# Attention and two MLPs on one core: tiles' homes in SBUF moved by steps of 32 bytes

## The chip, the cores and the metric

One core of a Trainium2 chip. The metric is device time in microseconds (us), the median of several executions. Engines: TensorE (PE; its weight loads are PEld), VectorE (DVE), ScalarE (ACT), GpSimd (POOL), and SyncE (SP), which issues the DMAs.

## The reference

Local attention over chunks of 32 queries (16 keys to the left, 8 to the right, 8 memory keys), then two MLPs over the 3072 tokens.

```python
scores = scale * np.matmul(q_c, k_full.transpose(0, 1, 3, 2))
...
x = np.ascontiguousarray(attn_out.transpose(0, 2, 1, 3)).reshape(B * S, H * D)
x = _moe_ref(x=x, **moe_kwargs)            # h = x @ w_in; g = silu(h); g @ w_out
return _moe2_ref(x=x, **moe2_kwargs)       # h = x @ w_in; g = relu(h)**2; g @ w_out
```

d_model is 512, d_ff is 2048, all in float32.

## The kernel before

Every float32 operand of the MLPs is kept as a high and a low part (fp32r), and a product is three matmuls: low by high, high by low, high by high. In each matmul one operand is *held* (128x128, loaded into the array) and one is *moving* (128 rows by 256 or 512 columns). In `nc.tensor.matmul(out, a, b)` a is held and b is moving.

Tokens are worked on in six blocks of 512. Blocks 0 and 1 go through the first MLP plainly: the hidden matmuls hold w_in (tiles i and d) under the moving tokens x0 or x1 (even blocks in x0, odd ones in x1); the back matmuls (`mlp`, lines 1250 to 1252) hold w_out (tiles o and u) under moving g. Blocks 2 to 5 have the same hidden matmuls, while the second half of the first MLP is done by a scheme with seven products of half-size blocks in place of eight; `multiply` (line 1585) issues them, with w held and g moving. The second MLP uses the seven-product scheme in both halves, for 48 pairs of weight blocks over six token blocks: `visit` (line 1403) multiplies the weight forms (held; tiles i, d, o and u2) with forms of the tokens (moving; tiles rv, rv, rq and four in x1), and `multiply` has g held and w moving (tiles wraw and wu; the fourth product in x0). Hidden matmuls: 6 blocks x 16 x 12 = 1152 of 512 columns, half of them in even blocks. Of the products over one pair of weights, 42 matmuls, 12 are over rv, 6 over rq and 24 over x1.

`multiply` swaps the two operands for the first layer:

```python
held, moving = g[:, at, a], w[:, wat, c]
if layer == 0:
    held, moving = moving, held
```

The order of all instructions on every engine is written out in ORDER; no planner runs.

Each tag has a pool, and pools stand in SBUF one behind the other in the order in which they are opened, each as long as its number of buffers times its largest tile. Slices of a tile used by a matmul start at multiples of 512 bytes from the tile's start. So where a tile starts, modulo some power of two, is set by the pools before it. Before: u0, u1, u2 (8320 bytes each), a gap of 64 bytes, then rq, pr, pts, xq, x0, x1, wraw, wu, wr, y (all multiples of 2048 bytes), a gap of 64, then i, d, o, g (multiples of 4096), rv (two of 4160), nm, sm. Homes in bytes modulo 256, from the start of the first pool, before and after the change:

```
tile                       before   after
rq                          192       32
x1, odd token blocks        192       96   (starts 64 into its tile)
x1, second MLP's tokens     192       32
x0                          192      128
wraw, wu                    192        0
i, d, o                       0      128
u0, u2                        0      128
u1                          128        0
g                             0       32
rv, first of a block          0       64   (starts 64 into its tile)
rv, second                   64       64

moving over held           before   after   (moving minus held, -128 to 128)
hidden, even: x0 over i, d  -64        0
hidden, odd: x1 over i, d   -64      -32
back: g over o, u0, u2        0      -96
back: g over u1             128       32
first-layer out: g over o     0      -96
first-layer out: g over x0   64      -96
products: x1, rq over forms -64      -96
products: first rv            0      -64
products: second rv          64      -64
second-layer out: wraw, wu over g  -64  -32
second-layer out: x0 over g       -64   96
```

Of the kernel before, what the change touches and what calls it, by code (L numbers as in the profile page):

```python
# [12 lines left out]
F32 = mybir.dt.float32  # L13
F32R = mybir.dt.float32r
# [15 lines left out]
TB = UG * GQ  # L30
# [4 lines left out]
P = 128  # L35
KT = DM // P
# [22 lines left out]
HALF2 = T2 // 2  # L59
# [11 lines left out]
WARM, DENSE = 512, 9  # L71
KEEP = 0
PLAIN, OUTS = 2, 10

# [249 lines left out]
def chunk_attention_two_mlps(ctx, tc, head, units, weights, out):  # L326
# [3 lines left out]
    def pool(tag, n=1, space=None):  # L330
        kw = {} if space is None else {"space": space}
        bufs[tag] = n
        pools[tag] = ctx.enter_context(tc.tile_pool(name=tag, bufs=n, **kw))
        return pools[tag]
# [1 line left out]

    moving = (
        ("rq", 1), ("pr", 1), ("pts", 1), ("xq", 3), ("x0", 1), ("x1", 1), ("wraw", 2),  # L340
        ("wu", 4), ("wr", 3), ("y", 2),
    )
    held = [(f"i{i}", 1) for i in range(FT) if i not in JOINED]
    held += [(f"d{i}", 1) for i in range(len(JOINED) // 2)] + [(f"o{i}", 1) for i in range(OUTS)]

    def gap(tag):
        pool(tag).tile([P, 16], F32, tag=tag, name=tag)

    for tag in ("u0", "u1", "u2"):
        pool(tag)  # L350
    gap("gap0")
    for tag, n in moving:
        pool(tag, n)
    gap("gap1")
    for tag, n in (*held, ("g", 3), ("rv", 2), ("nm", 3), ("sm", 4)):
        pool(tag, n)
    for tag, n in (("acc", 4), ("ph", 2), ("sc", 2)):
        pool(tag, n, bass.MemoryType.PSUM)
# [9 lines left out]
    def f(ap):  # L368
        return ap.bitcast(F32)

    def take(b, shape, dtype, name=None):
        b.tile = pools[b.tag].tile(shape, dtype, tag=b.tag, name=name or b.tag)
        return b.tile
# [22 lines left out]
    a = G.add({"DVE": 0.3}, -100.0, fill, new=[ones])  # L396
    a = G.add({"PE": 3.9}, -100.0, warm, [a], new=[dense], uses=[ones])
# [14 lines left out]
    for n in range(KEEP):  # L412
        a = G.add({"PE": 0.45}, 100.0, keep, [a], uses=[dense, ones])
# [12 lines left out]
    def step_due(j, i):  # L426
        if j == 0:
            return FIRST + SLOW * i / FT
        if j < PLAIN:
            return FIRST + SLOW + (j - 1) * BLOCK1 + i * STEP1  # L430
        return FIRST + SLOW + (PLAIN - 1) * BLOCK1 + (j - PLAIN) * BLOCKW + i * BLOCKW / FT
# [374 lines left out]
    def split_x(j, p, po, done, due):  # L806

        new = []
        if j not in x_buf:
            x_buf[j] = G.buf(f"x{j % 2}")  # L810
            x_done[j] = []
            new = [x_buf[j]]
        xb = x_buf[j]

        def tokens(c):
            t = xb.tile[:, c, p]
            return t if j < ON_PE else t.rearrange("p (g c q) -> p g c q", g=UG, c=GC)

        def made():
            return po.tile if j < ON_PE else po.tile.rearrange("p c g q -> p g c q")  # L820

        def x_high(e):
            if new:
                take(xb, [P, 2, KT, TB], F32R)
            nc.scalar.copy(tokens(0), made())  # L825

        def x_low(e):
            nc.vector.tensor_tensor(tokens(1), made(), f(tokens(0)), op=ALU.subtract)  # L828

        a = G.add({"ACT": 0.60}, due - 1, x_high, [*done, *x_done[j]], new=new, uses=[po, xb])  # L830
        x_done[j].append(G.add({"DVE": 0.7}, due, x_low, [a], uses=[po, xb],
                               port=j >= ON_PE))
# [470 lines left out]
    def tokens(b, due):  # L1303

        t0 = b * T2
        after, xf = stored[b], G.buf("x0")
        loads = []

        def form(n):
            return xf.tile[:, n]  # L1310

        for n, (k, half) in enumerate(((0, 0), (2, 0), (2, 1), (0, 1))):
            def load(e, n=n, k=k, half=half):
                if n == 0:
                    take(xf, [P, 7, 2, HALF2], F32, "xf")
                at = t0 + half * HALF2
                nc.sync.dma_start(
                    out=xf.tile[:, n],
                    in_=y1[k:k + 2, :, at:at + HALF2].rearrange("k p t -> p k t"),
                )  # L1320

            p = G.add({"SP": 0.45}, due - 50 + n, load, after, new=[xf] * (n == 0),
                      uses=[xf] * (n > 0), size=P * T2 * 4)
            p.behind += loads[:1]
            p.release = due - 50
            loads.append(p)

        def sums(o, a, b, after, at):
            def emit(e):
                engine[e].tensor_tensor(form(o), form(a), form(b), op=ALU.subtract)  # L1330

            p = G.add({"DVE": 0.70, "POOL": 1.30}, at, emit, after, uses=[xf], port=True)
            p.release = due - 40
            return p

        b11, b21, b22, b12 = loads
        t1 = sums(4, 3, 0, [b12, b11], due - 20)
        t3 = sums(3, 2, 3, [b22, t1], due - 18)
        t2 = sums(5, 2, 4, [b22, t1], due - 18)
        t4 = sums(6, 5, 1, [t2, b21], due - 16)  # L1340
        ready = {0: b11, 1: b21, 2: b22, 3: t3, 4: t1, 5: t2, 6: t4}
        xs, four = {}, []
        need = [1.5 * rank for rank in range(7)]
        for rank, n in enumerate(X_FORM[p] for p in PRODUCTS):

            shared, at = rank > 2, max(0, rank - 3)
            new = not four or not shared
            if shared:
                four = four or [G.buf("x1")]
                x = four[0]  # L1350
            else:
                x = G.buf(("rv", "rv", "rq")[rank])

            def high(e, n=n, x=x, new=new, shared=shared, at=at):
                if new:
                    take(x, [P, 4 if shared else 1, 2, 2, HALF2], F32R, "xs")
                nc.scalar.copy(x.tile[:, at, 0], form(n))

            def low(e, n=n, x=x, at=at):
                t = x.tile[:, at]  # L1360
                engine[e].tensor_tensor(t[:, 1], form(n), f(t[:, 0]), op=ALU.subtract)

            a = G.add({"ACT": 0.60}, due - 3 + need[rank], high,
                      [ready[n]] + ([] if new else [x.by]),
                      new=[x] * new, uses=[xf] + [x] * (not new))
            xs[n] = (x, at, G.add({"DVE": 0.70, "POOL": 1.30}, due - 2 + need[rank], low, [a],
                                  uses=[xf, x], port=True))
        return xs
# [579 lines left out]
    for j in range(PLAIN):  # L1948
# [3 lines left out]
        else:  # L1952
# [4 lines left out]
            for k in range(PAIRS):  # L1957
                at = step_due(j, 1) + k * 11 * STEP1 / PAIRS
                convert_out(0, k, at)
                if k in WORK0:  # L1960
                    what, m = jobs.pop(0)
                    what(m, at + 10)
        y, rest = mlp(j)
# [89 lines left out]
```

## Time and profile before

| | |
|---|---|
| median of 3 runs | 1060.7 us (1060.2 to 1060.95) |
| the profiled execution | 1067.14 us |
| its span, first to last instruction | 1065.3 us |
| PE busy | 1051.2 us, 99% |
| PEld busy | 960.8 us, 90% |
| DVE busy | 827.3 us, 78% |
| ACT busy | 600.4 us, 56% |
| POOL busy | 266.9 us, 25% |
| mean granted TensorE clock | 0.997 |

Engines work side by side, so the shares add to more than one. Matmuls are pipelined: the next starts long before the last has ended, and a busy PE need not be at its peak.

### The profile page before, as it was taken

What the parts mean: (1) busy time and instruction counts of PE and PEld (TensorE: products, weight loads), DVE (VectorE), ACT (ScalarE), POOL (GpSimd) and SP (SyncE); (2) the same over time, 40 slices, a digit from 0 to 9 for tenths busy, and PEclk for the clock granted to TensorE, in tenths of its full rate; (3) what the DMA queues carried; (4) which work ended last, traced back from release to release, by engine and by line L of the source; (5) the groups of instructions that cost most, each with busy time, mean ns of one, the idle gap of its engine ahead of it and who ended that gap; (6) DMA issues with size and microseconds to landing.
All of it is one profiled execution on the core that took longest, in us unless ns stands there. A gap on an engine that the chain in (4) does not pass through costs nothing.

```text
span 1065.3 us, 24883 instructions
## 1 busy us (share of the span) xinstructions
PE 1051.2 (99%) x9801; PEld 960.8 (90%) x9801; DVE 827.3 (78%) x1608; ACT 600.4 (56%) x1106; POOL 266.9 (25%) x246
## 2 busy tenths in 40 slices
PE   7999999999999999999999999999999999999998
PEld 5778777778888888988989999999999999999998
DVE  6779767667888788897888877777777778777766
ACT  4898755557676777766567544335335334335333
POOL 3231123132334332420210321221221222221210
PEclk9899999999999999999999999999999999999999
DMA  8777686989798879887674875766776667667675
GB/s 292 272 246 229 227 283 226 294 258 318 238 306 279 281 257 303 279 305 248 212 233 145 275 222 181 247 215 201 241 218 210 210 215 221 205 210 226 200 237 176
DMA packets 139603, 256.80 MB, mean 241 GB/s; under 512 B 12128, under 2 KB 52192, under 8 KB 139488
## 3 DMA queue, kind: packets, MB, share of 16 engines
q1 hardware_dynamic: 139488, 255.23, 73.5%
q8 instruction: 77, 1.26, 0.5%
q14 instruction: 38, 0.31, 0.1%
HBM read 202.75 MB, written 52.43 MB: 240 GB/s over the span
## 4 chain that ended last, share of the span: by engine, by line
PE 91%; DVE 3%; DMA 3%; ACT 2%; issue 1%; POOL 0%; SPq 0%; DVEq 0%; ACTq 0%
PE out L1585 35%; PE pp L1403 20%; PE ph L1191 8%; PE ph L1192 8%; PE ph L1193 8%; PE acc L1250 3%; PE acc L1252 3%; PE acc L1251 3%; PE sc L519 1%; PE po L737 1%; DVE g L1465 1%; DMA xf<-y 1%; DMA blocks<-head 1%; DMA i<-weights 1%; DMA w2s<-ws 1%
## 5 line engine op out<-in xcount | busy, mean ns | idle before, releaser
L1403 PE MATMUL pp<-xs,forms 128*128 128x256 f32 x2016 | 269.2, 279 | 1.4 <-DVE kept L1429 1.0
L1585 PE MATMUL out<-w,g 128*128 128x256 f32 x2016 | 264.4, 278 | 0.1
L1403 PEld LDWEIGHTS pp<-xs,forms 128*128 128x128 f32 x2016 | 249.8, 188 | 2.3 <-DVE kept L1429 2.2
L1585 PEld LDWEIGHTS out<-w,g 128*128 128x128 f32 x2016 | 246.8, 188 | 0.3 <-DVE g L1465 0.3
L1461 ACT CAST g<-sums 128x512 fp32r<-128x512 f32 x240 | 148.0, 619 | 118.7 <-PE out L1585 91.5
L1465 DVE TENSOR_TENSOR g<-sums,g 128x512 fp32r<-128x512 f32 x201 | 155.1, 776 | 35.7 <-ACT g L1461 34.4
L1585 PE MATMUL out<-g,w 128*128 128x256 f32 x1344 | 173.3, 284 | 1.1 <-POOL g L1465 0.9
L1585 PEld LDWEIGHTS out<-g,w 128*128 128x128 f32 x1344 | 166.9, 191 | 6.2 <-POOL g L1465 1.1
L1420 ACT ACTIVATE sums<-pp 128x256 f32<-128x256 f32 x192 | 73.9, 385 | 160.2 <-PE pp L1403 120.5
L1446 POOL TENSOR_TENSOR sums<-sums 128x256 f32<-128x256 f32 x68 | 59.6, 880 | 289.9 <-DVE sums L1446 234.8
L1191 PE MATMUL ph<-x,i 128*128 128x512 f32 x240 | 96.9, 404 | 2.1 <-ACT x L825 1.9
L1192 PE MATMUL ph<-x,i 128*128 128x512 f32 x240 | 96.0, 400 | 0.5 <-DVE x L828 0.5
L1193 PE MATMUL ph<-x,i 128*128 128x512 f32 x240 | 95.6, 398 | 0.0
L1439 DVE SCALAR_TENSOR_TENSOR sums<-sums 128x256 f32<-128x256 f32 x144 | 69.0, 484 | 20.3 <-ACT sums L1420 18.7
L1465 POOL TENSOR_TENSOR g<-sums,g 128x512 fp32r<-128x512 f32 x39 | 51.1, 1313 | 103.2 <-ACT g L1461 103.0
L1446 DVE TENSOR_TENSOR sums<-sums 128x256 f32<-128x256 f32 x172 | 70.8, 431 | 5.7 <-ACT sums L1543 4.7
L1642 ACT CAST w<-w 128x512 fp32r<-128x512 f32 x100 | 59.1, 619 | 24.0 <-PE out L1585 18.1
L1648 DVE TENSOR_TENSOR w<-w,w 128x512 fp32r<-128x512 f32 x88 | 62.5, 736 | 10.0 <-ACT w L1642 9.1
L1429 DVE TENSOR_TENSOR sums<-pp,sums 128x256 f32<-128x256 f32 x96 | 40.2, 419 | 24.1 <-PE pp L1403 23.7
L1191 PEld LDWEIGHTS ph<-x,i 128*128 128x128 f32 x240 | 45.5, 190 | 13.7 <-ACT x L825 2.3
L1191 PE MATMUL ph<-x,d 128*128 128x512 f32 x144 | 57.7, 401 | 0.0
L1192 PE MATMUL ph<-x,d 128*128 128x512 f32 x144 | 56.8, 395 | 0.0
(136 smaller groups left out, 1574.8 us busy)
## 6 DMA issues: line engine op xcount, KB each, us to landing
w<-w2s SPq DMA_DIRECT2D x120, 512.0 KB, 4.0
w<-w1s SPq DMA_DIRECT2D x32, 768.0 KB, 5.2
w<-w2s SPq DMA_DIRECT2D x96, 256.0 KB, 3.3
wraw<-weights SPq DMA_DIRECT2D x44, 512.0 KB, 5.0
raw<-units SPq DMA_DIRECT2D x20, 768.0 KB, 5.7
w2s<-ws SPq DMA_DIRECT2D x56, 256.0 KB, 3.2
raw<-units SPq DMA_DIRECT2D x20, 520.0 KB, 6.0
bounce<-squares SPq DMA_DIRECT2D x32, 256.0 KB, 4.0
```

The costliest lines, as they stand in the source:

```text
L1191: nc.tensor.matmul(o, w[:, 1, ws], x[:, 0, kt], start=(kt == 0), stop=False)
L1192: nc.tensor.matmul(o, w[:, 0, ws], x[:, 1, kt], start=False, stop=False)
L1193: nc.tensor.matmul(o, w[:, 0, ws], x[:, 0, kt], start=False, stop=(kt == KT - 1))
L1403: nc.tensor.matmul(o[:, at], w[:, a, ws], t[:, c, kt], start=first and kt == 0 and r == 0, stop=kt == 1 and r == 2, skip_group_check=True,)
L1420: nc.scalar.activation(t[:, to], q.bank[bank].tile[:, h], func)
L1439: nc.vector.scalar_tensor_tensor(t, t, 0.0, t, op0=ALU.max, op1=ALU.mult)
L1446: engine[e].tensor_tensor(q.t.tile[:, to], a[0].tile[:, a[1]], b[0].tile[:, b[1]], op=op)
L1461: nc.scalar.copy(take(g, [P, 2, 2, HALF2], F32R, "g2")[:, :, 0], read())
L1465: engine[e].tensor_tensor(t[:, :, 1], read(), f(t[:, :, 0]), op=ALU.subtract)
L1585: nc.tensor.matmul(out_, held[:, ms], moving, start=first and r == 0 and (m == 0 or alone is not None), stop=last and r == 2, skip_group_c ...
L1642: nc.scalar.copy(take(w, [P, m, 2, HALF2], F32R, "w2")[:, :, 0], raw.tile[:, at:at + m])
L1648: engine[e].tensor_tensor(t[:, :, 1], raw.tile[:, at:at + m], f(t[:, :, 0]), op=ALU.subtract)
```

## The change

The pools are opened in another order, with one gap of 32 bytes in place of two of 64; the tokens of odd blocks start 64 bytes into a tile that is 96 bytes longer; and the first rv of a token block starts 64 bytes into its tile, which is no longer than the largest of its tag. No instruction is added, removed or moved in the order.

```diff
+GAP, STEP = 8, 24
...
-    moving = (
-        ("rq", 1), ("pr", 1), ("pts", 1), ("xq", 3), ("x0", 1), ("x1", 1), ("wraw", 2),
-        ("wu", 4), ("wr", 3), ("y", 2),
-    )
     held = [(f"i{i}", 1) for i in range(FT) if i not in JOINED]
     held += [(f"d{i}", 1) for i in range(len(JOINED) // 2)] + [(f"o{i}", 1) for i in range(OUTS)]
 
-    def gap(tag):
-        pool(tag).tile([P, 16], F32, tag=tag, name=tag)
-
-    for tag in ("u0", "u1", "u2"):
-        pool(tag)
-    gap("gap0")
-    for tag, n in moving:
+    for tag, n in (("wraw", 2), ("wu", 4), ("wr", 3), ("y", 2), ("pr", 1), ("pts", 1), ("xq", 3)):
         pool(tag, n)
-    gap("gap1")
-    for tag, n in (*held, ("g", 3), ("rv", 2), ("nm", 3), ("sm", 4)):
+    pool("gap").tile([P, GAP], F32, tag="gap", name="gap")
+    for tag, n in (
+        ("g", 3), ("rq", 1), ("x1", 1), *held, ("x0", 1), ("u0", 1), ("u1", 1), ("u2", 1), ("rv", 2),
+        ("nm", 3), ("sm", 4),
+    ):
         pool(tag, n)
...
         def x_high(e):
-            if new:
+            if new and xb.tag == "x1":
+                t = take(xb, [P, STEP + 2 * KT * TB], F32R)[:, 16:16 + 2 * KT * TB]
+                xb.tile = t.rearrange("p (a k t) -> p a k t", a=2, k=KT)
+            elif new:
                 take(xb, [P, 2, KT, TB], F32R)
...
                 if new:
-                    take(x, [P, 4 if shared else 1, 2, 2, HALF2], F32R, "xs")
+                    m, step = 4 if shared else 1, 16 * (rank == 0)
+                    t = take(x, [P, step + m * 4 * HALF2], F32R, "xs")[:, step:]
+                    x.tile = t.rearrange("p (n a k t) -> p n a k t", n=m, a=2, k=2)
```

## Rows read from the trace of the kernel before

**Rows 1.** The page: busy time by engine, and the chain by engine.
```profile
PE 1051.2 (99%) x9801; PEld 960.8 (90%) x9801; DVE 827.3 (78%) x1608; ACT 600.4 (56%) x1106; POOL 266.9 (25%) x246
...
PE 91%; DVE 3%; DMA 3%; ACT 2%; issue 1%; POOL 0%; SPq 0%; DVEq 0%; ACTq 0%
```

**Rows 2.** Waits of PE: total us, times, longest; the longest in total.
```profile
PE sc L605 <- DMA blocks<-head: 1.9, 3, 0.9
...
PE ph L1191 <- ACT x L825: 1.9, 1, 1.9
```

**Rows 3.** Three stretches: length, then busy us (instructions) of PE, PEld, DVE, ACT, POOL.
```profile
396.00:581.00 185.00, 185.00 (x1495) 164.73 (x1494) 155.93 (x288) 126.53 (x236) 39.75 (x36) 1.00 0.75 250
581.00:822.00 241.00, 240.61 (x2067) 239.95 (x2066) 188.38 (x377) 109.20 (x227) 58.17 (x49) 1.00 0.68 218
822.00:1065.00 243.00, 238.51 (x2059) 237.92 (x2057) 179.68 (x358) 96.48 (x199) 49.99 (x44) 1.00 0.68 214
```

**Rows 4.** Groups by line and form: count, busy us, mean ns, idle before.
```profile
L1403 PE MATMUL pp<-xs,forms 128*128 128x256 f32 x2016 | 269.2, 279 | 1.4 <-DVE kept L1429 1.0
L1585 PE MATMUL out<-w,g 128*128 128x256 f32 x2016 | 264.4, 278 | 0.1
...
L1585 PE MATMUL out<-g,w 128*128 128x256 f32 x1344 | 173.3, 284 | 1.1 <-POOL g L1465 0.9
```

**Rows 5.** The chain in order of time: start us, us, line, merged count.
```profile
502.40 4.31 PE out L1585 x36
...
613.38 2.12 PE pp L1403 x18
...
668.66 2.13 PE pp L1403 x18
...
672.20 2.83 PE out L1585 x24
...
679.97 1.41 PE out L1585 x12
...
682.10 1.38 PE out L1585 x12
...
684.87 1.36 PE out L1585 x12
...
692.35 2.10 PE pp L1403 x18
...
746.18 2.10 PE pp L1403 x18
...
749.64 2.72 PE out L1585 x24
...
753.04 2.04 PE out L1585 x18
...
787.98 0.39 ACT sums L1420
...
794.92 0.97 PE pp L1403 x6
```

**Rows 6.** Timeline of PE: hidden matmuls, first and last of 22 in a row.
```profile
507.02 0.39 PE L1193 MATMUL ph<-x,i 128*128 128x512 f32 x1
...
511.92 0.39 PE L1193 MATMUL ph<-x,i 128*128 128x512 f32 x1
```

**Rows 7.** Timeline of PE: back matmuls, of 24 over u1, of 12 over o7.
```profile
206.04 0.40 PE L1250 MATMUL acc<-g,u 128*128 128x512 f32 x1
...
211.39 0.40 PE L1252 MATMUL acc<-g,u 128*128 128x512 f32 x1
...
233.03 0.39 PE L1250 MATMUL acc<-g,o 128*128 128x512 f32 x1
...
235.52 0.39 PE L1252 MATMUL acc<-g,o 128*128 128x512 f32 x1
```

**Rows 8.** DMA issues: queue, count, KB each, median us to landing.
```profile
raw<-units SPq DMA_DIRECT2D x20, 768.0 KB, 5.7
```

More of the change, by code (lines that the diff above doesn't have):

```diff
@@ L1352, in tokens, with high @@
                 x = G.buf(("rv", "rv", "rq")[rank])
-            def high(e, n=n, x=x, new=new, shared=shared, at=at):
+            def high(e, n=n, x=x, new=new, shared=shared, at=at, rank=rank):
                 if new:
-                    take(x, [P, 4 if shared else 1, 2, 2, HALF2], F32R, "xs")
+                    m, step = 4 if shared else 1, 16 * (rank == 0)
+                    t = take(x, [P, step + m * 4 * HALF2], F32R, "xs")[:, step:]
+                    x.tile = t.rearrange("p (n a k t) -> p n a k t", n=m, a=2, k=2)
                 nc.scalar.copy(x.tile[:, at, 0], form(n))
```

## The prediction

> **What bounds the kernel now.** Read first the page's busy shares and the chain that ended last [rows 1]: PE is busy in 99% of the span, and 91% of the chain runs through it. The longest of PE's waits is 1.9 us [rows 2], and the stretches show PE busy in all of 396 to 581 us and in nearly all from 581 us on [rows 3]. So there is next to no idle time to win; what can change is the time from one matmul's start to the next, which I call its pace. The groups [rows 4] give counts and shapes, but no pace: their 278 ns is the pipelined length of one. The pace stands in the chain, where consecutive matmuls are merged: a piece's time through its count.
>
> For 128x256 matmuls there are three paces. A piece of first-layer output matmuls, g over held w, takes 4.31 us for 36, 119.7 ns each [rows 5]. A piece of second-layer output matmuls, w over held g, takes 1.41 us for 12 in one place, 117.5 ns, and 1.36 us for 12 a little later, 113.3 ns; twenty-four take 2.83 or 2.72 us, 117.9 or 113.3 ns each [rows 5]. The instructions are the same kind and shape, and nothing waits in these pieces. Of the products, L1403, a pair issues eighteen in a row over rv, rv and rq: they take 2.12 or 2.13 us in a slow stretch and still 2.10 in a quick one, where eighteen output matmuls take 2.04 [rows 5]. Either pace is kept: of the eighteens, the seven in the chain from 613.38 to 668.66 us are all slow, the six from 692.35 to 746.18 all quick.
>
> For 128x512 the hidden matmuls start 4.90 us apart over 21 steps, 233.3 ns each [rows 6]. The plain back matmuls take 2.49 us over 11 steps, 226.4 ns, with an o tile held; but 24 over u1 take 5.35 us over 23 steps, 232.6 ns [rows 7].
>
> Now lay the homes table of the kernel's section beside this, with distance = moving home minus held home, on a circle of 256 bytes. The pace 119.7 belongs to 0, 113.3 and 117.5 belong to -64, the slow eighteen have one third each at 0, +64 and -64. At 512 columns 0 has 226.4, -64 has 233.3, and u1, the only held tile at 128, has 232.6 where the o tile at 0 has 226.4. That u1 differs is why I keep 256 bytes and a sign, not 128: on a circle of 128 u1 would be at 0 too. The weights of the next matmul are loaded while this one streams (PEld is busy 237.92 of 243 us, [rows 3]), so both read SBUF together, and where they start seems to set how often they meet. The paces are read from rows; that distance is their cause is inferred, since the stages differ in more than that.
>
> **The change, part by part.** No instruction is added or dropped: the order is written out, the queues keep every DMA, no wait is new. Two views into longer tiles cost nothing. The whole sum is homes. What a distance not seen so far (-96, -32) costs I bound by the lowest and highest pace seen at that width.
>
> 1. First-layer output, g over w: 0 to -96. Of the 1344, 48 hold x0 and are left aside: 1296. The nearest row is -64, with 113.3 and 117.7 (the mean of 117.5 and 117.9); I take the middle, 115.5. (119.7 - 115.5) x 1296 = -5.4 us; ends 113.3 and 119.7: -8.3 to 0.
> 2. Second-layer output, w over g, 2016: -64 to -32 (288 of them, over x0, to +96). The present mean first: the last two stretches hold 4126 matmuls in 479.12 us of busy PE [rows 3], 116.1 ns each; 576 of those are over rv, at about 118 (that is 2.10 us less six of rq at 113.3, through 12), which leaves 115.8 for the others. -32 lies as near to 0 as to -64, so I take the middle of the ends 113.3 and 119.7: 116.5, or +0.7 x 2016 = +1.4 us; ends -5.0 to +7.9.
> 3. Products over x1 and rq, 1440: -64 to -96. Nearest is where they are: 0 us; ends 113.3 and 119.7: -3.6 to +5.6.
> 4. Products over rv, 576: 0 and +64 both to -64, a distance that has rows: 118 to 115.8, -1.3 us; ends -2.7 to 0.
> 5. Hidden, 576 in even token blocks: -64 to 0. At 0 the back matmuls show 226.4 in a stretch that keeps its pace; that every stretch does I don't assume, and count 229: (233.3 - 229) x 576 = -2.5 us; ends -4.0 and 0.
> 6. Hidden, 576 in odd blocks: -64 to -32, the middle of 226.4 and 233.3, 229.9: -2.0 us; ends -4.0 and 0.
> 7. Plain back, 384: 0 to -96, between -64 (233.3) and 128 (232.6), so about 233 for the 229 above: +1.5 us; ends 0 and +1.7. The 48 of them over u1 go to +32 and are counted with the rest.
>
> Sum -5.4 + 1.4 + 0 - 1.3 - 2.5 - 2.0 + 1.5 = -8.3 us. The profiled execution took 1067.14 us, 1.84 of them outside its span; it stands 6.4 us above the median of the runs, 1060.7. It would go to 1058.8, and the median to 1052.4.
>
> What takes a part back: PE in time needs its operands in time. DVE is busy 155.93 of 185 us in the first layer and less after that [rows 3], so a pace 3% quicker leaves it room. At the starts of token blocks the chain leaves PE for about 7 us, from ACT at 787.98 to the products at 794.92 [rows 5], while PE works on; a PE 1% quicker there arrives 0.1 us too soon, at each of five token blocks. I count nothing; without that cover it is 0.5 us. The raw loads now land in rq 32 bytes past a multiple of 64; they are due 50 us or more ahead in the code and take 5.7 us [rows 8], so even twice that would be covered.
>
> **A rule against it.** The row first: 119.7 ns against 113.3 for one shape, both without a wait [rows 5]. The Trainium skill ("TensorE: Matmul & The Clock Gate", Step-by-step: what each phase is for) says that TensorE has two independent SBUF read ports and that loading the next weights doesn't steal read bandwidth from the running matmul. By that rule alone homes would not matter, and the time would stay at 1060.7. The trace speaks against it without refuting it, since other things than homes differ between these stages.
>
> **The rivals.** *A, the quick pace everywhere.* The new distances let all 128x256 matmuls settle at 113.3: the low ends of 1, 2 and 3 are -8.3 - 5.0 - 3.6 = -16.9, with 4 to 7 as counted (-4.3) -21.2 us, 1039.5. For it: 113.3 exists, is held over many pairs, and once a slow stretch turned quick inside a run with no wait (1.41, 1.38, 1.36 for 12, [rows 5]). Against: two distances must both do it.
>
> *B, 32 bytes from 0 is as bad as 0.* -32 and -96 lock at 119.7 like the first layer's output. Then 1 gains nothing, 2 and 3 lose 7.9 and 5.6, and with -4.3 the sum is +9.2: 1069.9. For it: the only neighbour at 32 bytes of -32 on one side is the worst pace seen. Against: no row of -32 or -96 exists. With L the common pace of the 4752 matmuls of 1 to 3, the sum is zero where 1296 (L - 119.7) + 2016 (L - 115.8) + 1440 (L - 115.8) = 4300 ns, so at L = 117.8: the slow pace at -64, held all the time, already eats the gain. Above that the change loses.
>
> *C, homes are not the cause.* The pace is set by the stage (which operand is fresh, which banks are written), and the stretches keep theirs: 1060.7. For it: at -64 there are two paces without a change of distance. Against: within one line the eighteen over rv and rq are slower than their neighbours.
>
> **How the numbers follow.** Chances: the forecast (from -3 to -14 us) 0.42, A 0.20, B 0.22, C 0.16. About 0.2% (2 us) is what a measurement can tell from none. Faster by more: forecast and A, and little of C, which by mere shifts can go either way (0.02): 0.64. The same: 0.11 of C and 0.02 of B, where L is near 117.8: 0.13. Slower: 0.20 of B and 0.03 of C: 0.23. The predicted time is the forecast's, 1052.4. All low ends give -8.3 - 5.0 - 3.6 - 2.7 - 4.0 - 4.0 + 0 = -27.6 us, all high ones 0 + 7.9 + 5.6 + 0 + 0 + 0 + 1.7 = +15.2. The range reaches past A's point by 3 us and past B's by 1.5, until about 1 in 10 is left out on either side: 1036.5 to 1071.4. The forecast's own range is 1047 to 1058.
>
> **What would show it.** In the chain after: pieces of 36 in the first layer at about 4.16 us (A: 4.08, B: 4.31); pieces of 12 in the second at 1.36 to 1.41, without 1.44; the eighteen down towards 2.04; hidden steps of 226 to 229 ns in even and about 230 in odd blocks; back steps up to about 233. PE's waits should stay under 2 us each. I am wrong if -32 or -96 locks above 117.8, if the paces don't move at all, or if PE's gain comes back as waits at the starts of token blocks.

## The result and the profile after

The kernel became slower: 1069.38 us in the median of 6 runs (1067.49 to 1072.28), against 1061.19 us in 6 runs of the kernel before beside it (1060.2 to 1065.08). The ratio is 1.0075 [1.0052, 1.0097]. The forecast was 1052.4. The profiled execution took 1068.93 us with a span of 1067.1.

The page after, its busy times by engine and three of its groups (out<-in, count, busy us and mean ns of one, idle before):

```profile
PE 1054.2 (99%) x9801; PEld 966.3 (91%) x9801; DVE 827.5 (78%) x1608; ACT 600.2 (56%) x1106; POOL 266.7 (25%) x246
...
L1402 PE MATMUL pp<-xs,forms 128*128 128x256 f32 x2016 | 271.5, 281 | 1.1 <-DVE kept L1428 1.0
L1584 PE MATMUL out<-w,g 128*128 128x256 f32 x2016 | 270.7, 281 | 0.1
...
L1584 PE MATMUL out<-g,w 128*128 128x256 f32 x1344 | 171.7, 282 | 1.6 <-POOL g L1464 1.0
```

Beside [rows 1] nothing but PE and its weight loads (PEld) has grown, by 3.0 and 5.5 us, and PE's idle time is as small as it was. In the groups, against [rows 4], the second layer's output went from 264.4 to 270.7 us, the products from 269.2 to 271.5, the first layer's output from 173.3 to 171.7. So the loss lies in the two stages for which the prediction counted +1.4 and, for the products, 0 and -1.3.

Windows of the second MLP, to lay beside the last two of [rows 3]:

```profile
581.00:822.00 241.00, 239.98 (x2027) 239.13 (x2026) 183.52 (x370) 105.06 (x218) 57.05 (x48) 1.00 0.67 216
822.00:1065.00 243.00, 241.50 (x2044) 241.03 (x2042) 178.65 (x357) 95.43 (x196) 49.11 (x43) 1.00 0.67 211
```

PE is as busy, the granted clock is 1.00 in both, but 481.48 us of work hold 4071 matmuls, 118.3 ns each, where it was 116.1. The chain shows it piece by piece (start us, us, line, merged count):

```profile
486.58 4.28 PE out L1584 x36
...
663.68 2.13 PE pp L1402 x18
667.22 2.85 PE out L1584 x24
670.78 2.13 PE out L1584 x18
...
746.59 2.85 PE out L1584 x24
750.14 2.13 PE out L1584 x18
...
1050.87 12.49 PE out L1584 x105
```

A piece of 24 in the second layer takes 2.85 us, at 667 as at 746: 118.8 ns. In [rows 5] it was 2.83 and then 2.72. No piece of outputs, or of products over x1 and rq, reaches 113.3 any more; a few over rv, now at -64, do. The last 105 take 119.0 each. The first layer's 36 went from 4.31 to 4.28 us, 118.9 ns, not to the 4.16 that was forecast.

The timeline of PE: first and last of 24 back matmuls over o, of 24 hidden ones in an even block, of 24 in an odd block:

```profile
151.59 0.39 PE L1247 MATMUL acc<-g,o 128*128 128x512 f32 x1
...
156.97 0.40 PE L1249 MATMUL acc<-g,o 128*128 128x512 f32 x1
...
480.94 0.39 PE L1188 MATMUL ph<-x,i 128*128 128x512 f32 x1
...
486.19 0.39 PE L1190 MATMUL ph<-x,i 128*128 128x512 f32 x1
...
500.55 0.40 PE L1188 MATMUL ph<-x,i 128*128 128x512 f32 x1
...
505.91 0.40 PE L1190 MATMUL ph<-x,i 128*128 128x512 f32 x1
```

Over 23 steps each: back 233.9 ns (226.4 over o7 in [rows 7]), hidden even 228.3, hidden odd 233.0 (233.3 in [rows 6]). Even blocks gained, odd ones did not.

The table below lays the order of all matmuls beside their starts in the trace and takes the mean time to the next start, by what moves over what is held; steps longer than 130 ns (256 columns) or 250 ns (512) are left out: waits, and matmuls at a lower granted clock. "Us" is the sum over the stage, after minus before.

```
                            before          after          us
first layer, g over w       119.5 (0)       118.1 (-96)   -1.7
second layer, w over g      115.3 (-64)     118.3 (-32)   +5.2
second layer, x0 over g     115.1 (-64)     119.6 (+96)   +1.3
products, x1 and rq         115.5 (-64)     117.6 (-96)   +3.0
products, rv                118.2 (0, +64)  116.7 (-64)   -0.8
hidden, even                233.5 (-64)     228.4 (0)     -2.75
hidden, odd                 233.5 (-64)     233.2 (-32)   -0.2
back, g over o, u0, u2      229.0 (0)       233.8 (-96)   +1.5
```

That sums to +5.6 us. The two profiled executions are only 1.8 apart, since the steps left out are 2.8 us shorter in the one after, all of it where the first token block starts; about 1 us is in neither. Windows of that place, before and after (the columns of [rows 3], then the granted clock, DMA share and GB/s):

```profile
28.00:34.00 6.00, 5.48 (x12) 3.89 (x13) 3.68 (x6) 5.50 (x9) 2.76 (x2) 0.50 0.79 303
...
28.00:34.00 6.00, 6.00 (x87) 4.70 (x87) 5.26 (x7) 5.87 (x11) 3.14 (x3) 1.00 0.64 227
```

In the execution of the kernel before, the granted clock was 0.50 there, the level of 1.2 GHz, after PE had waited 1.9 us for ACT [rows 2], and ten hidden matmuls in a row started 427 ns apart in place of 233. In the one after it was 1.00. So the prediction's base held some 2.3 us of lower clock, an estimate from these steps, which is no part of what the homes do.

### The profile page after: what moved, and what is told of

It reads as the page before. It is cut to its first block, busy times and chain, and to the rows that moved or that the text cites. A ratio compares the mean times of both kernels' runs of the same rounds, so it can differ in the third digit from the quotient of the medians.

```text
span 1067.1 us, 24883 instructions
## 1 busy us (share of the span) xinstructions
PE 1054.2 (99%) x9801; PEld 966.3 (91%) x9801; DVE 827.5 (78%) x1608; ACT 600.2 (56%) x1106; POOL 266.7 (25%) x246
## 4 chain that ended last, share of the span: by engine, by line
PE 91%; DMA 3%; DVE 2%; ACT 2%; POOL 1%; issue 1%; SPq 0%; ACTq 0%; DVEq 0%; POOLq 0%
PE out L1584 35%; PE pp L1402 21%; PE ph L1188 8%; PE ph L1190 8%; PE ph L1189 8%; PE acc L1247 3%; PE acc L1249 3%; PE acc L1248 3%; PE sc L513 1%; PE po L731 1%; DMA i<-weights 1%; DMA w<-w1s 1%; DMA w<-w2i 1%; DMA xf<-y 1%; DVE g L1464 1%
## 5 line engine op out<-in xcount | busy, mean ns | idle before, releaser
L1402 PE MATMUL pp<-xs,forms 128*128 128x256 f32 x2016 | 271.5, 281 | 1.1 <-DVE kept L1428 1.0
L1584 PE MATMUL out<-w,g 128*128 128x256 f32 x2016 | 270.7, 281 | 0.1
L1584 PEld LDWEIGHTS out<-w,g 128*128 128x128 f32 x2016 | 252.3, 188 | 0.3 <-DVE g L1464 0.3
L1584 PE MATMUL out<-g,w 128*128 128x256 f32 x1344 | 171.7, 282 | 1.6 <-POOL g L1464 1.0
L1419 ACT ACTIVATE sums<-pp 128x256 f32<-128x256 f32 x192 | 73.8, 385 | 164.6 <-PE pp L1402 117.7
L1188 PE MATMUL ph<-x,i 128*128 128x512 f32 x240 | 95.5, 398 | 1.5 <-ACT x L822 0.8
L1189 PE MATMUL ph<-x,i 128*128 128x512 f32 x240 | 94.3, 393 | 0.5 <-DVE x L825 0.5
L1190 PE MATMUL ph<-x,i 128*128 128x512 f32 x240 | 94.4, 393 | 0.0
L1188 PE MATMUL ph<-x,d 128*128 128x512 f32 x144 | 57.5, 399 | 0.0
L1190 PE MATMUL ph<-x,d 128*128 128x512 f32 x144 | 56.6, 393 | 0.0
L1189 PE MATMUL ph<-x,d 128*128 128x512 f32 x144 | 56.5, 393 | 0.0
```

The lines of the kernel that those rows point to most:

```text
L1188: nc.tensor.matmul(o, w[:, 1, ws], x[:, 0, kt], start=(kt == 0), stop=False)
L1189: nc.tensor.matmul(o, w[:, 0, ws], x[:, 1, kt], start=False, stop=False)
L1190: nc.tensor.matmul(o, w[:, 0, ws], x[:, 0, kt], start=False, stop=(kt == KT - 1))
L1402: nc.tensor.matmul(o[:, at], w[:, a, ws], t[:, c, kt], start=first and kt == 0 and r == 0, stop=kt == 1 and r == 2, skip_group_check=True,)
L1419: nc.scalar.activation(t[:, to], q.bank[bank].tile[:, h], func)
L1584: nc.tensor.matmul(out_, held[:, ms], moving, start=first and r == 0 and (m == 0 or alone is not None), stop=last and r == 2, skip_group_c ...
```

## The experiments

The theory after the result: a matmul's pace is set by where the moving tile starts relative to the held tile that is being loaded, each stage by itself, and the quick pace of 113.3 ns is not to be had at -32 and -96. Against it stood: the stages couple (a slow one carries its pace into the next); the order of the pools or something else in the change, not the distances; waits and mere variation between executions.

**Second layer alone back to -64 (wg64).**

```diff
-GAP, STEP = 8, 24
+GAP, STEP = 16, 24
...
-        ("nm", 3), ("sm", 4),
+        ("nm", 3), ("sm", 3),
```

> The changed kernel with one distance put back: second-layer output, wraw and wu over g, at -64 instead of -32 (the gap is 64 bytes, and the tag sm has 3 buffers instead of 4 to make room); all other distances as in the changed kernel. Theory 1, distance sets the pace: the 1728 matmuls go from 118.3 ns back to between 115.3 (the mixed pace of before) and 113.3, so 5 to 9 us less than the changed kernel: 1061 to 1064. Rival 2, each stage's pace is pulled along by the stages beside it, since the slow and the quick state pass from one run of matmuls to the next: with the products still at -96 the output matmuls stay near 117.5, and the time stays within 3 us of 1069. Rival 3, not distance but something else in the new order of the pools (other engines' or DMAs' addresses): 1069.

Measured: 1064.81 us in 12 runs, 1.0022 [0.9999, 1.0045] against 1064.36 for the kernel before on that chip. The chain:

```profile
657.64 1.38 PE out L1584 x12
...
663.24 2.06 PE pp L1402 x18
...
666.72 2.80 PE out L1584 x24
...
670.22 2.08 PE out L1584 x18
```

Eighteen outputs take 2.08 instead of 2.13 us; over the whole stage w over g is down from 118.3 to 116.1 ns, while the products over x1 and rq, at 118.1, and the first layer, at 118.1, gained nothing. This one edit took back more than half of the loss. Some 3.8 us of that are w over g; another 1.8 came from the products over rv, which went from 116.7 to 113.7 ns though their own distance stayed at -64.

**Products alone back to -64 (prod64).**

```diff
-GAP, STEP = 8, 24
+GAP, STEP = 8, 16
...
+    pool("g", 3)
+    pool("gap2").tile([P, 8], F32, tag="gap2", name="gap2")
     for tag, n in (
-        ("g", 3), ("rq", 1), ("x1", 1), *held, ("x0", 1), ("u0", 1), ("u1", 1), ("u2", 1), ("rv", 2),
+        ("rq", 1), ("x1", 1), *held, ("x0", 1), ("u0", 1), ("u1", 1), ("u2", 1), ("rv", 2),
...
-                t = take(xb, [P, STEP + 2 * KT * TB], F32R)[:, 16:16 + 2 * KT * TB]
+                t = take(xb, [P, STEP + 2 * KT * TB], F32R)[:, 8:8 + 2 * KT * TB]
```

> The changed kernel with one distance put back: products over x1 and rq at -64 instead of -96 (a second gap of 32 bytes between g and rq, x1 longer by 64 instead of 96 bytes, its odd tokens 32 bytes into it); w over g stays at -32, all else as in the changed kernel. Theory 1: the 1440 matmuls go from 117.6 to between 115.5 and 113.3 ns, 3 to 6 us less: 1063 to 1066. Rival 2: they stay near 117.6 beside output matmuls at 118.3, and the time stays within 3 us of 1069. Rival 3: 1069.

Measured: 1065.16 us in 12 runs, 1.0015 [0.9993, 1.0037]. The chain:

```profile
656.37 0.68 PE pp L1404 x6
...
658.47 0.71 PE pp L1404 x6
...
660.60 1.39 PE pp L1404 x12
...
662.70 2.04 PE pp L1404 x18
...
666.13 2.85 PE out L1586 x24
669.70 2.13 PE out L1586 x18
...
1046.71 12.51 PE out L1586 x105
```

The mirror image: every eighteen of products takes 2.04 us (113.3 ns each, rv's among them), and the outputs between them keep 2.85 and 2.13. Quick and slow pieces alternate within a few microseconds, at a granted clock of 0.998 for the run, so a slow stage does not drag the next one down: coupling in that form is refuted as the cause of the loss. But the shorter pieces over x1, at the same -64, are quick or slow by their place: six take 0.68 or 0.71 us, twelve 1.39, and this repeats from one pair of weights to the next, so that x1 and rq together come to 115.9 ns only. At -64 what stands before a piece has a say.

**All 256-column stages to 64 bytes, hidden to 0 (all64).**

```diff
-GAP, STEP = 8, 24
+GAP, STEP = 16, 16
```

> The changed kernel with gap and pad of 64 bytes each: every 128x256 matmul at -64 (only w in x0 over g at +64), first-layer output included, which was at 0 before and at -96 after; hidden matmuls at 0 in even and odd blocks. Theory 1: against the kernel before with its quick pace (about 1060): first-layer output from 119.5 to between 117.7 and 113.3 (-2 to -8 us), hidden from 233.4 to about 228.5 (-5.5 us), back matmuls +1.5, x0 over g +1: 1049 to 1055. Rival 2 gives the same, as no stage is left at a bad distance. Rival 3, the order of the pools itself costs: 1064 or more, the hidden matmuls alone being quicker.

Measured: 1060.29 us in 12 runs, 0.9977 [0.9954, 0.9999], under the change by a per cent but short of what was expected. The chain:

```profile
494.38 4.24 PE out L1584 x36
...
658.35 2.12 PE pp L1402 x18
661.88 2.79 PE out L1584 x24
```

Here every eighteen of products, at the same -64 as in prod64, takes 2.12 us, 117.8 ns, from the first to the last. The first layer's 36 take 4.24 in one go, 117.8. Where matmuls of the attention (sc) break a piece in two it goes another way; in the chain, and then the timeline of PE from the break on:

```profile
406.00 1.41 PE out L1584 x12
407.41 0.79 PE sc L513 x53
...
408.35 2.78 PE L1584 MATMUL out<-g,w 128*128 128x256 f32 x23
```

Twelve before the break are slow; the 23 behind it start within 2.50 us (the last alone takes 0.28), 113.6 ns each. Of the 20 pieces of this stage with such a break, 19 end at 113.3, and all 11 without one stay at 117.7 to 117.9. So -64 permits the quick pace and does not grant it: which of the two holds is settled at the entry into a piece. Over the stage the first layer's output comes to 116.0 ns (119.5 before), but w over g to 115.9 and the products over x1 and rq to 117.3, slower than before's 115.3 and 115.5. Hidden matmuls at 0 gave 228.1 and 227.6 ns.

**Matmuls alone, by distance (ladder).** The kernel does none of the reference's work: it loads one tile, issues three-matmul groups of each width, and moves only the start of the moving tile, by 32 bytes a time, first without a wait, then with a reader of PSUM after each segment. In that second pass four matmuls of 512 columns at distance 0 stand before each segment of 256 columns from 32 to 288; only from 320 on is there a wait.

```diff
+                    h0 = 512 * at + 256 * a + 128 * k
+                    m0 = d // 4 + 512 * at + 256 * c
+                    nc.tensor.matmul(
+                        narrow[:, k], h[:, h0:h0 + 128], m[:, m0:m0 + 256],
+                        start=r == 0, stop=r == 2, skip_group_check=True,
+                    )
...
+            for d in DISTANCES:
```

> Only matmuls, no part of the reference: 48 of 128x256 and 36 of 128x512 at each distance from 0 to 480 bytes by 32, with the hi and lo pattern of the kernel; once straight through, once with a wait before each distance. The output is left meaningless. Theory 1: at 256 columns 120 ns at 0, 113.3 or 118 at 192 (that is -64), 117 to 120 at 160 and 224 (-96 and -32); at 512 columns 226.7 at 0 and 233 at 192; the same again 256 bytes on. If 128 bytes were the period, 64 and 192 would agree. Rival 3: no dependence on the distance, one pace throughout. Rival 2: the straight pass differs from the one with waits, since the state is carried from one distance to the next.

Mean ns to the next start in the second half of each segment, by distance; the next turn of 256 bytes gave the same in the first and third line, to about 0.1 ns:

```
moving - held      0      32     64     96     128    160    192    224
256, no wait     120.0  117.7  117.8  120.2  118.5  118.7  117.8  118.3
256, second pass 120.0  116.7  117.7  120.2  118.9  117.4  113.35 118.2
512, no wait     226.7  233.4  228.7  233.5  233.6  234.5  233.3  233.2
```

The chain of its second pass, 48 narrow matmuls at 96, 160, 192 and 256 (0), then 36 wide ones at 224, 256 (0), 288 (32) and 320 (64); each piece of 48 begins with one step of some 225 ns, each of 36 with one of some 340:

```profile
260.23 5.88 PE narrow L43 x48
...
273.79 5.76 PE narrow L43 x48
...
280.48 5.58 PE narrow L43 x48
...
293.70 5.89 PE narrow L43 x48
...
404.60 8.67 PE wide L53 x36
...
414.04 8.45 PE wide L53 x36
...
423.26 8.68 PE wide L53 x36
...
432.71 8.53 PE wide L53 x36
```

Nothing differs between the pieces of one width but the address, so it does set the pace, and rival C falls. The ladder moves the moving tile alone; that the distance counts and not that tile's own home, the kernels show: x0 and w_in both at 128 gave 228.4 ns (after), both at 0 gave 228.2 (hid_only, below). Without waits the circle is 256 bytes. -32 (224) and -96 (160) are at 118.3 and 118.7, near what the stages after show (118.3, and 117.6 to 118.1). And 192, which is -64, has two paces here as well: 117.8 without waits, 113.35 in the second pass. In that pass 64 itself kept 117.7, while 320, the same distance a turn further, came to 113.35, and 448, that of 192, kept 117.8. Two more differ by the turn: 128 had 118.9 and then 120.0, 160 had 117.4 and then 118.9. No distance but 64 and -64 went below 116.6. At 512 columns only 0 and 64 are quick.

**The two kernels once more (before_again, after_again).** No edit.

> The kernel before, profiled once more, nothing changed. Theory 1 with two paces at -64: its runs spread from 1056.6 to 1067.1 us because stretches of the second layer keep now the quick pace, now the slow one; so this profile's share of pieces at 113.3 ns differs from the first profile's, and the execution's time with it, about 0.0045 us for each matmul that changes pace; the 512-column matmuls and the first layer's output at distance 0 keep 233.5, 229 and 119.5 ns within 0.2. Rival 4, the spread is waits or DMA: the paces stay as in the first profile and the idle time of PE differs.

> The changed kernel once more, beside the others of this call. Theory 1: 0.5 to 0.9% over the kernel before; its own runs lie closer together than those of before, for at -32 and -96 there is no quick pace to fall into. Rival 4: as wide a spread as before's 10 us.

Measured: 1061.5 us for the one execution of before, which is 5.6 below the one in the prediction's rows; after 1070.25 us in 6 runs (1067.76 to 1071.32), 1.0062 [1.0041, 1.0083] against 1063.81. The chain of the kernel before in the prediction's execution:

```profile
824.18 2.13 PE pp L1403 x18
827.72 2.83 PE out L1585 x24
```

and in the new one:

```profile
820.55 2.10 PE pp L1403 x18
824.01 2.72 PE out L1585 x24
```

The same place in the order is slow in one execution and quick in the other. Of the 36 eighteens of products in either chain from 600 us on, 17 were quick then and 25 now. The stage w over g went from 115.3 to 114.5 ns, the products over x1 and rq from 115.5 to 114.8. With the smaller stages that makes 2.7 of the 5.6 us; another 2.8 lie where the first token block starts: the granted clock, 0.50 from 28 to 34 us in the prediction's execution, is 1.00 there in this one (some 2.3 us), and PE waits 1.2 us for ACT in place of 1.9. So the base of the prediction's sum was one draw among several. The kernel after, in contrast, repeats its paces to about 0.1 ns; at -32 and -96 no second pace was seen in it. That its runs lie closer together than before's is not shown: they spread over 3.6 us, against 8.1 in before's 22 runs, but in the first comparison, 6 runs each, over 4.8 against 4.9. Between these two executions the matmuls of the table make +8.6 us, the steps left out -1.2, and the spans differ by 6.2.

**Hidden in even blocks alone (hid_only).** The kernel before, with its x0 pool moved to distance 0:

```diff
-        ("rq", 1), ("pr", 1), ("pts", 1), ("xq", 3), ("x0", 1), ("x1", 1), ("wraw", 2),
-        ("wu", 4), ("wr", 3), ("y", 2),
+        ("rq", 1), ("pr", 1), ("pts", 1), ("xq", 3), ("x1", 1), ("wraw", 2),
+        ("wu", 4), ("wr", 3), ("y", 2), ("x0", 1),
...
-    gap("gap1")
...
-            if new:
+            if new and xb.tag == "x0":
+                t = take(xb, [P, 16 + 2 * KT * TB], F32R)[:, 16:]
+                xb.tile = t.rearrange("p (a k t) -> p a k t", a=2, k=KT)
+            elif new:
```

> The kernel before with one part of the change alone: tokens of even blocks over w_in at distance 0 instead of -64 (x0 last among the moving tags, 64 bytes longer in place of the second gap, its tokens 64 bytes into it); every other distance as before. Theory 1: 576 matmuls from 233.5 to about 228.4 ns, -2.9 us or -0.3%, the paces of the second layer as mixed as before's. If only the second layer mattered: no difference.

Measured: 1060.4 us in 12 runs, 0.9972 [0.9955, 0.9988]. The timeline of PE, first and last of 24 hidden matmuls of an even block:

```profile
482.16 0.40 PE L1193 MATMUL ph<-x,i 128*128 128x512 f32 x1
...
487.40 0.39 PE L1195 MATMUL ph<-x,i 128*128 128x512 f32 x1
```

That is 227.8 ns a step, and 228.2 over all even blocks, -2.9 us; odd blocks stay at 233.5. This part of the change is worth about 0.3% by itself, and the second layer's losses buried it.

**Held tiles at one home, moving ones 64 bytes off (two_homes).** From the kernel before, with one gap of 64 bytes: wraw and wu at 64 below the g they run over; g, rq and x1 64 above the held weights; rv 64 below them; hidden at 0 in even and +64 in odd blocks.

```diff
+GAP = 16
...
+    for tag, n in (("wraw", 2), ("wu", 4), ("wr", 3), ("y", 2), ("pr", 1), ("pts", 1), ("xq", 3)):
+        pool(tag, n)
+    for tag, n in (*held, ("x0", 1), ("u0", 1), ("u1", 1), ("u2", 1), ("rv", 2)):
         pool(tag, n)
-    gap("gap1")
-    for tag, n in (*held, ("g", 3), ("rv", 2), ("nm", 3), ("sm", 4)):
+    pool("gap").tile([P, GAP], F32, tag="gap", name="gap")
+    for tag, n in (("g", 3), ("rq", 1), ("x1", 1), ("nm", 3), ("sm", 4)):
...
+                    m, step = 4 if shared else 1, 16 * (rank == 0)
+                    t = take(x, [P, step + m * 4 * HALF2], F32R, "xs")[:, step:]
+                    x.tile = t.rearrange("p (n a k t) -> p n a k t", n=m, a=2, k=2)
```

> Homes from the ladder: held tiles, x0, wraw and wu together at 0, g, rq and x1 64 above them, rv 64 below, one gap of 64 bytes. Then every 128x256 matmul is at 64 or -64 (g over o +64, w over g -64, x1 and rq over forms +64), hidden matmuls at 0 in even blocks and +64 in odd ones, back matmuls at +64. Theory 1, from the ladder's 228.7 at +64 and 226.7 at 0: back 233.3 to 229 (-1.4 us) and hidden in odd blocks 227.6 to 229 (+0.8 us) against the version with all at -64, otherwise as that one: 0.1 to 0.6% under the kernel before, depending on how much of it keeps the quick pace. Were the sign of 64 to matter, g over o and the products would settle at 118 and the time at that of before or above.

Measured: 1058.27 us in 11 runs (1055.66 to 1062.08), 0.9952 [0.9937, 0.9967]: faster than both kernels. The chain:

```profile
485.62 4.24 PE out L1580 x36
495.36 4.08 PE out L1580 x36
504.94 9.52 PE out L1580 x84
...
1039.30 12.38 PE out L1580 x105
```

The first layer's output at +64 runs at 117.8 ns in the last pieces until 490 us and at 113.3 from 495 on, and keeps that until 572 us, where products begin to stand between its pieces. Over the stage it is 116.4 (before 119.5), hidden 228.5 and 229.2, products 115.5. The second layer's w over g had 116.4 in this execution, the slow pace for much of it, so this version does not have the quick pace throughout either.

## Why the prediction was wrong

It saw the right cause: the distance of moving and held tile, on a circle of 256 bytes; the sign matters in the ladder at 512 columns (64 and -64: 228.7 and 233.3 ns), while at 256 columns both have the same two paces. It was wrong in what it put at the two distances that had no row, -32 and -96: it read the pace there as a middle between neighbours, forecast a gain of 8.3 us, and the time rose by 8.2.

**Part 2 is the step that failed most.** "-32 lies as near to 0 as to -64, so I take the middle" gave 116.5 and +1.4 us; measured were 118.3, and 119.6 for the x0 product at +96, together +6.5. Pace was no smooth function of distance, from which a middle could be read. The 113.3 in the present mean comes from a quick pace that the ladder shows at 64 and -64 alone, so the step from -64 to -32 or -96 lost it.

**Part 3 failed in the same way.** "Nearest is where they are: 0 us" took the mean of two paces, 115.8, as a property of the neighbourhood. At -96 no quick pace was seen: 117.6 here, 118.1 in wg64, 117.4 to 118.9 in the ladder. That cost +3.0 us.

**Part 1** had the sign and was mis-sized: 118.1 in place of 115.5, -1.7 us in place of -5.4. Again the middle of -64's two paces was lent to -96.

**Part 6** took the middle at 512 columns: 229.9 forecast for -32, 233.2 measured, -0.2 us in place of -2.0. In the ladder 0 and 64 are quick and the six others lie between 233.2 and 234.5.

**Parts 4, 5 and 7** held; each of them ends at a distance, or on a plateau, that the trace had shown. rv at -64: 116.7 for 115.8, -0.8 for -1.3; that the size came near is luck, for at the same -64 rv had 113.7 in wg64, 114.1 in prod64 and 117.3 in all64. Hidden even at 0: 228.4 for 229, -2.75 for -2.5, and by itself in hid_only -2.9. Back at -96: 233.8 for 233, +1.5 as counted.

**The base.** The prediction transferred its sum from the profiled execution to the median of the runs. That is not neutral. The execution held some 2.3 us of lower clock, and with before at -64, 115.3 ns in it is a mix of two paces whose shares change from one execution to the next, and the second profile had 114.5. What is lost at -32 and -96 is counted from the mix, so +5.6 us from one execution and +8.6 from the other, where the median of the runs rose by 8.2.

**The rivals.** B named the mechanism that decided, -32 and -96 holding a pace above 117.8. That its time, 1069.9, is close is luck: it took 119.7 where 118.1 was measured, the mean over the matmuls of parts 1 to 3. With 118.1 its formula gives +1.7 us; the rest came from part 6 and from the base. A is refuted, no stage of its parts 1 to 3 reached 113.3. C is refuted by the ladder, by wg64 against prod64, and by hid_only. That PE's gain would come back as waits played no part: there was no gain, and PE's idle time did not grow.

The rule of the Trainium skill ("TensorE: Matmul & The Clock Gate", Step-by-step: what each phase is for), that loading the next weights takes no read bandwidth from the running matmul, cannot be read to mean that homes don't matter for this kernel's float32 pairs: with nothing changed but the address, 48 matmuls took 5.58 or 5.89 us in the ladder. Whether it is read bandwidth that the bad distances cost, no run shows.

What stays open: which entry leads to which of the two paces at 64 bytes. In all64 the break by the attention's matmuls turned 19 of 20 pieces quick; in two_homes, at +64, the same break left 18 of 20 slow, and the unbroken pieces turned quick where the even block's hidden matmuls (at 0) give way to the odd block's (at +64): the three before are slow, the eight behind quick. In the kernel before, the stretch that turned quick at 682 us [rows 5] did so right behind six matmuls over rv at distance 0. No run changes the entry alone. So the theory that each stage goes by itself holds for the loss at -32 and -96, but not at 64 bytes, where the neighbours have a part. Why 0 is among the worst distances for 256 columns and the best for 512 was not tried either.

## What to carry to other kernels

When PE has no idle time, look for its pace, time through count in the chain, and compare it between stages of the same shape. Before moving homes measure all distances in a bare ladder: here 256-column pairs did best at 64 bytes on either side (modulo 256), 512-column ones at 0, and a distance without a row must not be priced as the middle of its neighbours. Where one stage shows two paces, profile several executions before taking a mean as the base, and look at the granted clock of each stretch, not at its mean over the run.

## What the runs showed of the hardware

The pace of a matmul of the same kind and shape lay between 113.35 and 120.2 ns at 256 columns and between 226.7 and 234.5 at 512, in the ladder, where only the distance of two addresses changes; without waits it repeated every 256 bytes. At 64 and -64 there are two paces, 113.3 and 117.8, with the same program: a piece settles on one within some five matmuls of its entry and keeps it. In the kernel before, where moving and held tiles stand at -64 in products and outputs alike, a pace lasts over many pieces and changes between executions (17 or 25 quick eighteens of 36). Its time spread over 10.5 us in 29 runs on one chip (1056.61 to 1067.13). The paces are a part of that and the clock another: the five runs with a mean granted clock of 0.999 or more took 1058.8 us on average, the other 24 1064.2.
